# Five engine programs without a Block around them, and x's load behind GpSimd's first fills

## The chip, the cores and the metric

The kernel runs on one core of a Trainium2 chip. The metric is the device time of one execution in microseconds (us), and lower is better. A core has five engines that run their own instruction streams and meet only at semaphores: TensorE (PE; its weight loads are shown as PEld), VectorE (DVE), ScalarE (ACT), GpSimd (POOL) and SyncE (SP). SP and ACT also issue DMAs, each on a queue of its own (q1 and q10 in the profile); both queues are served by the same 16 DMA engines.

## What is computed

One decode step of a transformer block for 4 sequences, with a layer norm in front of two branches that run side by side and are added to x:

```python
def reference(A_x, A_k_cache, A_v_cache, A_wq, A_wo, B_x, B_w_gate, B_w_up, B_w_down):
    x = A_x                                  # (4, 1, 512)
    xn = _layernorm(x, axis=-1)
    # attention: 32 query heads, 8 key/value heads, the last 4096 of 16384 cache rows
    #   o = softmax((xn @ wq) . k * Dh**-0.5) . v ; return o @ wo
    # feed-forward: (silu(xn @ w_gate) * (xn @ w_up)) @ w_down
    return x + _A_ref(xn, A_k_cache, A_v_cache, A_wq, A_wo) + _B_ref(xn, B_w_gate, B_w_up, B_w_down)
```

All inputs are bfloat16. The parts of the two caches that are read are 32 MB each; the five weight matrices come to some 13 MB.

## The kernel before

**Staging.** The weights WQ, WG, WU, WD and WO have buffers of their own. The keys of one key/value head (4 sequences of 4096 rows, 4 MB) go into one buffer KB in two halves, the values into one buffer VB. There is one KB and one VB, so head r+1 can be loaded only where head r has been used.

**SP, the loads (L238 to L269).** SP issues WQ, WG, WU, then for each of the 8 heads the two halves of K (L245) and V (L250), WD after the first head (L263), at last WO in four parts (L253). A half of K waits until PE has transposed the same half of the head before (`s_tr`), V until PE has finished the product with the values of the head before (`s_pv`). At the end SP waits for the result (`s_y`), issues two of the four output DMAs, and waits until all four have landed (`wait_ge(d_out, 64)`, L269).

**POOL, the constants (L183 to L236).** POOL fills 17 tiles (L185 to L201), drains (L202), turns some of them into an identity, masks and selectors (`select`, L205), and raises `s_const` (L226); then it fills a few more and raises `s_zero` (L236).

**ACT (L271 to L297).** ACT issues the load of x (L273), takes the square root for the layer norm (L275), waits for `s_const`, issues four small loads of x in another layout (X4, L278), which are first used by the last addition, and then works through the heads: copies of transposed keys (L283) and exponentials (L286). It issues the other two output DMAs (L297).

**DVE (L299 to L377).** DVE waits for x, does the layer norm (L302 to L316, raising `s_xn`), copies the transposed x (L318) and the query (L320), does the feed-forward's activation (L362 to L368), then in each head copies of transposed keys (L330), maxima (L336) and the sums, and at the very end the addition of x (L377), which raises `s_y`.

**PE (L379 to L529).** PE waits for `s_const` and `s_xn`, transposes the normed x (L385), then waits for WQ and makes the query (L392), waits for WG and WU and makes gate and up (L399). Then comes a loop over the 8 heads: 16 chunks of transposed keys (L414) with the scores of the chunk two before (L427), the maximum and its shift (L434, L439), and the product with the values (L450, L455). In all heads but the first, extra matmuls without a use (`spin`, L467) stand between these steps. After the loop come the down projection and the output projection (L473, L477).

**The Block.** The five programs stand in one `with nc.Block() as block:` (L181). What the program makes of it: in front of each engine's instructions a branch to that engine's part, behind them a branch to a common end (line L181 in the profile), and in that end a barrier: each engine drains and counts up one semaphore, POOL waits until all four others have done so and releases them. A barrier of the same form stands ahead of the five programs (line L543); it belongs to the program's set-up and not to the Block.

Of the kernel before, what the change touches and what calls it, by code (L numbers as in the profile page):

```python
# [5 lines left out]
ALU = mybir.AluOpType  # L6
ACT = mybir.ActivationFunctionType
AX = mybir.AxisListType


def bass_parallel_sum__sliding_block_cached__swiglu_ffn__decode_kernel(
# [125 lines left out]
    d_v = sem("d_v")  # L137
    s_const = sem("s_const")
# [42 lines left out]
    with nc.Block() as block:  # L181

        @block.gpsimd  # L183
        def _(eng):
            eng.memset(ident[:], 0.0)  # L185
            eng.memset(I4[:], 0.0)
            eng.memset(ones[:], 1.0)
            eng.memset(own[:], 1.0)
            eng.memset(moff[:], 0.0)
            eng.memset(coff[:], 0.0)  # L190
            eng.memset(neg[:], 0.0)
            eng.memset(dq[:], 1.0)
            eng.memset(dr[:], 0.0)
            eng.memset(X4[:], 0.0)
            eng.memset(sel4[:], 0.0)
            eng.memset(guT[:].rearrange("p t b -> p (t b)"), 0.0)
            eng.memset(OP[:].rearrange("p t b -> p (t b)"), 0.0)
            eng.memset(sel[:], 0.0)
            eng.memset(head[:], 0.0)
            eng.memset(CM[:], 0.0)  # L200
            eng.memset(QT[:, HKV, :], 0.0)  # L201
            eng.drain()  # L202

            def select(t, pattern, op, fill, base, mult):
                eng.affine_select(t, t, pattern=pattern, compare_op=op, fill=fill, base=base,  # L205
                                  channel_multiplier=mult)
            select(I4[:], [[-1, B]], ALU.not_equal, 1.0, 0, 1)
            select(ident[:], [[-1, 128]], ALU.not_equal, 1.0, 0, 1)
            select(neg[:], [[-1, NH]], ALU.not_equal, -1.0, 0, 1)
            ownv = own[:].rearrange("k (j b) -> k j b", b=B)  # L210
            moffv = moff[:].rearrange("k (j b) -> k j b", b=B)
            coffv = coff[:].rearrange("k (b h) -> k b h", h=REP)
            select(ownv, [[0, NJ], [-REP, B]], ALU.is_ge, 0.0, 0, 1)
            select(moffv, [[0, NJ], [-REP, B]], ALU.is_ge, OFF, 0, 1)
            select(coffv, [[-REP, B], [0, REP]], ALU.is_ge, OFF, 0, 1)
            select(dq[:], [[-32, 4]], ALU.is_ge, 0.0, 0, 1)
            select(dr[:], [[-1, NR]], ALU.not_equal, 1.0, 0, 1)
            eng.drain()
            select(ownv, [[0, NJ], [REP, B]], ALU.is_ge, 0.0, REP - 1, -1)
            select(moffv, [[0, NJ], [REP, B]], ALU.is_ge, OFF, REP - 1, -1)  # L220
            select(coffv, [[REP, B], [0, REP]], ALU.is_ge, OFF, REP - 1, -1)
            select(dq[:], [[32, 4]], ALU.is_ge, 0.0, 31, -1)
            for a in range(1, 4):
                eng.drain()
                select(dr[:], [[-1, NR]], ALU.not_equal, 1.0, -32 * a, 1)
            eng.drain().then_inc(s_const, 1)  # L226

            for n in range(4):
                select(sel[:], [[-1, 32]], ALU.not_equal, 1.0, -32 * n, 1)
                select(head[:], [[0, 128]], ALU.not_equal, 1.0, -32 * n, 1)  # L230
                select(sel4[:], [[-1, B]], ALU.not_equal, 1.0, -32 * n, 1)
                eng.drain()
            eng.memset(dsum[:], 0.0)
            eng.memset(Osb[:], 0.0)
            eng.memset(P[:], 0.0)
            eng.drain().then_inc(s_zero, 1)  # L236

        @block.sync  # L238
        def _(eng):
            H = NT // 2  # L240

            def load_k(g, h):
                if g > 0:
                    eng.wait_ge(s_tr, NCH * (g - 1) + (h + 1) * NCH // 2)
                eng.dma_start(KB[:, h * H:(h + 1) * H, :], kv_ap(A_k_cache, g, h * H, (h + 1) * H)).then_inc(d_k[h], 16)  # L245

            def load_v(g):
                if g > 0:
                    eng.wait_ge(s_pv, g)
                eng.dma_start(VB[:], kv_ap(A_v_cache, g, 0, NT)).then_inc(d_v, 16)  # L250

            def load_wo(n, a, b):
                eng.dma_start(WO[:, a:b, :], wo_ap[:, a:b, :]).then_inc(d_wo[n], 16)  # L253

            eng.dma_start(WQ[:], wq_ap).then_inc(d_wq, 16)
            eng.dma_start(WG[:], wg_ap).then_inc(d_wg, 16)
            eng.dma_start(WU[:], wu_ap).then_inc(d_wu, 16)
            for g in range(HKV):
                load_k(g, 0)
                load_k(g, 1)  # L260
                load_v(g)
                if g == 0:
                    eng.dma_start(WD[:], wd_ap).then_inc(d_wd, 16)  # L263
            for q in range(4):
                load_wo(q, WOS[q], WOS[q + 1])
            eng.wait_ge(s_y, 1)
            for n in range(2):
                eng.dma_start(out_ap[n], y[32 * n:32 * n + B, :]).then_inc(d_out, 16)
            eng.wait_ge(d_out, 64)  # L269

        @block.scalar  # L271
        def _(eng):
            eng.dma_start(X[:], x_ap).then_inc(d_x, 16)  # L273
            eng.wait_ge(s_var, 1)
            eng.activation(st_std[:], st_var[:], ACT.Sqrt).then_inc(s_std, 1)  # L275
            eng.wait_ge(s_const, 1)
            for n in range(4):
                eng.dma_start(X4[32 * n:32 * n + B, :], x4_ap[n]).then_inc(d_x4, 16)  # L278

            def group(r):  # L280
                for n, c in enumerate(ACT_CH):
                    eng.wait_ge(s_tr, r * NCH + (c + 1))
                    eng.activation(KT[:, c % 4], kt_ps[c % 3], ACT.Copy).then_inc(s_ea, 1)  # L283
                for q in range(NB):
                    eng.wait_ge(s_mk, r * NB + (q + 1))
                    eng.activation(P[:, BT * q:BT * (q + 1), :], ps_S[q][:].rearrange("p (t n) -> p t n", n=NH),  # L286
                                   ACT.Exp, scale=SCALE).then_inc(s_p, 1)

            eng.wait_ge(s_gu, 1)
            eng.activation(ex[:], gate_ps.rearrange("p (t b) -> p t b", b=B), ACT.Exp, scale=-1.0).then_inc(s_ex, 1)  # L290
            with eng.Fori(0, HKV) as r:
                group(r)
            eng.wait_ge(s_e, 1)
            eng.activation(S2[:], acc4_ps[:], ACT.Copy).then_inc(s_ec, 1)  # L294
            eng.wait_ge(s_y, 1)
            for n in range(2, 4):
                eng.dma_start(out_ap[n], y[32 * n:32 * n + B, :]).then_inc(d_out, 16)  # L297

        @block.vector  # L299
        def _(eng):  # L300
            eng.wait_ge(d_x, 16)
            eng.tensor_reduce(st_sum[:], X[:], AX.X, ALU.add)  # L302
            eng.drain()
            eng.tensor_scalar(st_mean[:], st_sum[:], 1.0 / D, None, ALU.mult)
            eng.drain()
            eng.tensor_scalar(xc[:], X[:], st_mean[:, 0:1], None, ALU.subtract)
            eng.drain()
            eng.tensor_tensor(xsq[:], xc[:], xc[:], ALU.mult)
            eng.drain()
            eng.tensor_reduce(st_sum[:], xsq[:], AX.X, ALU.add)  # L310
            eng.drain()
            eng.tensor_scalar(st_var[:], st_sum[:], 1.0 / D, EPS, ALU.mult, ALU.add).then_inc(s_var, 1)
            eng.wait_ge(s_std, 1)
            eng.reciprocal(st_rstd[:], st_std[:])
            eng.drain()
            eng.tensor_scalar(xn[:], xc[:], st_rstd[:, 0:1], None, ALU.mult).then_inc(s_xn, 1)  # L316
            eng.wait_ge(s_xT, 1)
            eng.tensor_copy(XnT[:], xT_ps.rearrange("p (c b) -> p c b", b=B)).then_inc(s_xnT, 1)  # L318
            eng.wait_ge(s_q, 1)
            eng.tensor_copy(QT[:, 0:HKV].rearrange("p k (b h) -> p k b h", b=B),  # L320
                            q_ps.rearrange("p (k h b) -> p k b h", k=HKV, b=B))
            eng.drain()

            eng.tensor_copy(QC[:], QT[:, 0])

            def group(r, rest=None):
                for c in range(NCH):
                    if c not in ACT_CH:
                        eng.wait_ge(s_tr, r * NCH + (c + 1))
                        eng.tensor_copy(KT[:, c % 4], kt_ps[c % 3]).then_inc(s_ev, 1)  # L330
                    if c == 2 and rest:
                        rest()
# [37 lines left out]
            with eng.Fori(1, HKV) as r:  # L370
                group(r, lambda: norm(r - 1))
# [186 lines left out]
```

## Time and profile before

| | us |
|---|---|
| median of 3 runs | 197.28 (196.95 to 197.57) |
| the profiled execution, its own time | 196.62 |
| its span, first to last instruction | 194.9 |
| its mean granted TensorE clock | 0.982 of full speed |

The span and the rows of the trace are on one time scale, with zero at the first instruction. 196.62 - 194.9 = 1.72 us of the execution's own time lie ahead of the first or behind the last instruction that the trace shows. In the rows, DMA-issuing instructions stand under SPq and ACTq, a count of equal instructions behind "x", and in square brackets the idle time ahead of an instruction with what ended it. "us to landing" is counted from the issue to the last byte.

### The profile page before, as it was taken

The page shows a single profiled execution, that of the slowest core. Times are in us where ns is not written, and L with a number is a line of the kernel's source. Part 1 is how long each engine was busy: PE and PEld are TensorE (multiplying, and loading weights), DVE is VectorE, ACT ScalarE, POOL GpSimd, SP SyncE. Part 2 cuts the span into 40 slices and gives each one's busy share as a digit, 9 for nine tenths or more (in the row PEclk, how much of TensorE's full clock was granted, in tenths as well). Part 3 has the DMA queues.
Part 4 walks back from the last instruction along what each step waited for, and adds up shares of the span by engine and source line. Part 5 has one row for each costly group of instructions (what it writes and reads, how often), then busy time and mean ns, then how long its engine had stood idle before and what let it go on. Part 6 is the DMA issues. An engine that isn't in the chain of part 4 may idle for free.

```text
span 194.9 us, 8285 instructions
## 1 busy us (share of the span) xinstructions
PE 160.3 (82%) x3646; PEld 131.6 (68%) x3646; DVE 101.7 (52%) x217; ACT 61.1 (31%) x77; POOL 12.0 (6%) x51
## 2 busy tenths in 40 slices
PE   0137759958699979997999799979997999799984
PEld 0127759946698569856985597559756976697632
DVE  4200025870478348824882588258825882588230
ACT  2020002524064406440634063407340734073401
POOL 8870000000000000000000000000000000000000
PEclk9999999985999999999999999999999999999999
DMA  6999999999999999999999999999999999999991
GB/s 216 430 435 430 418 427 437 434 424 423 427 481 425 387 430 474 430 397 430 464 430 414 430 454 430 414 430 447 437 420 430 441 430 420 430 441 430 436 396 67
DMA packets 4688, 81.13 MB, mean 416 GB/s; under 512 B 580, under 2 KB 584, under 8 KB 968
## 3 DMA queue, kind: packets, MB, share of 16 engines
q1 hardware_dynamic: 4624, 81.01, 97.2%
q8 instruction: 6, 0.10, 0.2%
q10 hardware_dynamic: 56, 0.01, 0.0%
q14 instruction: 2, 0.02, 0.0%
HBM read 81.01 MB, written 0.00 MB: 416 GB/s over the span
## 4 chain that ended last, share of the span: by engine, by line
DMA 63%; PE 32%; DVE 2%; issue 1%; ACT 0%; SPq 0%; DVEq 0%
DMA kbuf<-in_A_k_cache_dram 52%; PE ps_kt L414 18%; DMA wu_sb<-in_B_w_up_dram 11%; PE ps_s L427 5%; PE ps_o L399 2%; PE ps_kt L467 2%; PE ps_s L473 1%; PE ps_o L463 1%; PE ps_o L450 1%; PE ps_o L462 1%; DVE kT L330 1%; PE ps_s L439 0%; PE ps_s L477 0%; DVE oP L374 0%; ACT s L294 0%
## 5 line engine op out<-in xcount | busy, mean ns | idle before, releaser
L414 PE MATMUL ps_kt<-ident,kbuf 128*128 128x128 bf16 x1024 | 76.5, 221 | 10.2 <-DMA kbuf<-in_A_k_cache_dram 8.2
L330 DVE COPY kT<-ps_kt 128x1024 bf16<-128x1024 bf16 x88 | 57.6, 686 | 21.6 <-PE ps_kt L414 21.6
L414 PEld LDWEIGHTS ps_kt<-ident,kbuf 128*128 128x128 bf16 x1024 | 59.2, 98 | 13.4 <-DMA kbuf<-in_A_k_cache_dram 13.4
L283 ACT ACTIVATE kT<-ps_kt 128x1024 bf16<-128x1024 bf16 x40 | 41.0, 1024 | 65.5 <-PE ps_kt L414 65.5
L427 PE MATMUL ps_s<-qC,kT 128*128 128x16 bf16 x1024 | 44.6, 170 | 3.1 <-DVE kT L330 2.1
L427 PEld LDWEIGHTS ps_s<-qC,kT 128*128 128x128 bf16 x1024 | 37.5, 97 | 4.6 <-DVE kT L330 4.1
L286 ACT ACTIVATE p<-ps_s 128x512 bf16<-128x512 f32 x32 | 16.5, 602 | 34.7 <-PE ps_s L439 34.7
L467 PE MATMUL ps_kt<-own,ones 128*128 128x512 bf16 x102 | 25.9, 380 | 0.0
L336 DVE TENSOR_REDUCE mx<-ps_s 128x16 f32<-128x512 f32 x32 | 22.0, 689 | 5.7 <-PE ps_s L427 3.6
L450 PEld LDWEIGHTS ps_o<-vbuf,p 128*32 128x32 bf16 x1024 | 17.8, 102 | 4.6 <-ACT p L286 4.6
L450 PE MATMUL ps_o<-vbuf,p 128*32 128x128 bf16 x1024 | 19.2, 228 | 0.3
L348 DVE COPY osb<-ps_o 128x128 f32<-128x128 f32 x8 | 2.3, 292 | 29.9 <-PE ps_o L455 29.9
L455 PE MATMUL ps_o<-p,ones 128*32 128x256 bf16 x64 | 17.0, 287 | 0.0
L467 PEld LDWEIGHTS ps_kt<-own,ones 128*128 128x128 bf16 x102 | 8.2, 98 | 8.2 <-issue 1.1
L439 PE MATMUL ps_s<-cm,own 128*128 128x512 bf16 x32 | 9.1, 411 | 1.0 <-DVE cm L345 1.0
L385 PE MATMUL ps_s<-i,xn 4*128 4x4 f32 x4 | 0.6, 261 | 9.2 <-POOLq L226 9.2
L385 PEld LDWEIGHTS ps_s<-i,xn 4*128 4x128 f32 x4 | 0.6, 206 | 9.2 <-POOLq L226 9.2
L455 PEld LDWEIGHTS ps_o<-p,ones 128*32 128x32 bf16 x64 | 6.5, 101 | 0.0
L439 PEld LDWEIGHTS ps_s<-cm,own 128*128 128x128 bf16 x32 | 2.6, 101 | 5.7 <-DVE cm L345 3.5
L392 PE MATMUL ps_s<-xnT,wq_sb 128*128 128x4 bf16 x128 | 3.6, 166 | 3.4 <-DMA wq_sb<-in_A_wq_dram 3.4
L392 PEld LDWEIGHTS ps_s<-xnT,wq_sb 128*128 128x128 bf16 x128 | 3.5, 104 | 3.5 <-issue 3.5
L362 DVE TENSOR_SCALAR ex<-ex 128x56 f32<-128x56 f32 x1 | 0.2, 192 | 9.1 <-ACT ex L290 9.1
(84 smaller groups left out, 77.4 us busy)
## 6 DMA issues: line engine op xcount, KB each, us to landing
kbuf<-in_A_k_cache_dram SPq DMA_DIRECT2D x16, 2048.0 KB, 14.1
vbuf<-in_A_v_cache_dram SPq DMA_DIRECT2D x8, 4096.0 KB, 16.5
wq_sb<-in_A_wq_dram SPq DMA_DIRECT2D x1, 4096.0 KB, 12.3
wo_sb<-in_A_wo_dram SPq DMA_DIRECT2D x1, 2816.0 KB, 22.6
wg_sb<-in_B_w_gate_dram SPq DMA_DIRECT2D x1, 1792.0 KB, 16.7
wu_sb<-in_B_w_up_dram SPq DMA_DIRECT2D x1, 1792.0 KB, 20.9
wd_sb<-in_B_w_down_dram SPq DMA_DIRECT2D x1, 1792.0 KB, 42.1
wo_sb<-in_A_wo_dram SPq DMA_DIRECT2D x1, 640.0 KB, 23.5
```

What stands on the lines that cost most here:

```text
L283: eng.activation(KT[:, c % 4], kt_ps[c % 3], ACT.Copy).then_inc(s_ea, 1)
L286: eng.activation(P[:, BT * q:BT * (q + 1), :], ps_S[q][:].rearrange("p (t n) -> p t n", n=NH), ACT.Exp, scale=SCALE).then_inc(s_p, 1)
L330: eng.tensor_copy(KT[:, c % 4], kt_ps[c % 3]).then_inc(s_ev, 1)
L336: eng.tensor_reduce(mx[:, q, :], ps_S[q][:].rearrange("p (t n) -> p n t", n=NH), AX.X, ALU.max)
L392: last = mm(q_ps[:, h * B:(h + 1) * B], WQ[:, c, h * Dh:(h + 1) * Dh], XnT[:, c, :], start=(c == 0 and h == 0), stop=(c == NC - 1), skip_g ...
L399: last = mm(o[:, t * B:(t + 1) * B], w[:].rearrange("p c (m t) -> p c t m", t=NF)[:, c, t, :], XnT[:, c, :], start=(w is WG and t == 0 and ...
L414: last = eng.transpose(kt_ps[c % 3][:, k, :], KB[:, CH * c + k, :], ident[:])
L427: last = mm(ps_S[q][:, NH * t:NH * (t + 1)], KT[:, c % 4, k, :], QC[:], start=(t == 0), stop=False, skip_group_check=True)
L439: mm(ps_S[q][:].rearrange("p (t n) -> p t n", n=NH), own[:], CM[:].unsqueeze(1).to_broadcast([128, BT, NH]), start=False, stop=True, skip_ ...
L450: mm(O_ps[32 * n:32 * n + 32, :], P[:, t:t + 2, :].rearrange("p t n -> p (t n)"), VB[:, t, :], start=(t < 4), stop=(t >= NT - 4), skip_gro ...
L455: last = mm(den_ps[32 * n:32 * n + 32, :], ones[:, 0:32], P[:, DT * e:DT * (e + 1), :].rearrange("p t n -> p (t n)"), start=False, stop=(e ...
L467: mm(ps_kt[k][:], ones[:], own[:].unsqueeze(1).to_broadcast([128, 4, 128]), skip_group_check=True)
```

## The change

The Block goes. Each engine's program becomes a plain function with the same body; the five are called one after another in the main program, in the order SP, POOL, ACT, DVE, PE. With the Block go its branches and the barrier at its end. The barrier of the set-up stays, and so does SP's last wait for the four output DMAs.

One wait is added: POOL's first drain, the one behind its 17 fills, raises a new semaphore `s_go`, and ACT waits for it before it issues the load of x. No other instruction, and no order on any engine, is changed. (The lines of the changed kernel are 2 to 5 lower than those of the kernel before.)

```diff
+    s_go = sem("s_go")
...
-    with nc.Block() as block:
-        @block.gpsimd
-        def _(eng):
+    def on_gpsimd(eng):
...
             eng.memset(QT[:, HKV, :], 0.0)
-            eng.drain()
+        eng.drain().then_inc(s_go, 1)
...
-        @block.scalar
-        def _(eng):
+    def on_scalar(eng):
+        eng.wait_ge(s_go, 1)
         eng.dma_start(X[:], x_ap).then_inc(d_x, 16)
...
+    on_sync(nc.sync)
+    on_gpsimd(nc.gpsimd)
+    on_scalar(nc.scalar)
+    on_vector(nc.vector)
+    on_tensor(nc.tensor)
```

More of the change, by code (lines that the diff above doesn't have):

```diff
@@ new lines, in on_sync, with load_k, load_v, load_wo @@
+    def on_sync(eng):
+        H = NT // 2
+        def load_k(g, h):
+            if g > 0:
+                eng.wait_ge(s_tr, NCH * (g - 1) + (h + 1) * NCH // 2)
+            eng.dma_start(KB[:, h * H:(h + 1) * H, :], kv_ap(A_k_cache, g, h * H, (h + 1) * H)).then_inc(d_k[h], 16)
+        def load_v(g):
+            if g > 0:
+                eng.wait_ge(s_pv, g)
+            eng.dma_start(VB[:], kv_ap(A_v_cache, g, 0, NT)).then_inc(d_v, 16)
+        def load_wo(n, a, b):
+            eng.dma_start(WO[:, a:b, :], wo_ap[:, a:b, :]).then_inc(d_wo[n], 16)
+        eng.dma_start(WQ[:], wq_ap).then_inc(d_wq, 16)
+        eng.dma_start(WG[:], wg_ap).then_inc(d_wg, 16)
+        eng.dma_start(WU[:], wu_ap).then_inc(d_wu, 16)
+        for g in range(HKV):
+            load_k(g, 0)
+            load_k(g, 1)
+            load_v(g)
+            if g == 0:
+                eng.dma_start(WD[:], wd_ap).then_inc(d_wd, 16)
+        for q in range(4):
+            load_wo(q, WOS[q], WOS[q + 1])
+        eng.wait_ge(s_y, 1)
+        for n in range(2):
+            eng.dma_start(out_ap[n], y[32 * n:32 * n + B, :]).then_inc(d_out, 16)
+        eng.wait_ge(d_out, 64)
@@ new lines, in on_scalar, with group @@
+    def on_scalar(eng):
+        eng.wait_ge(s_go, 1)
+        eng.dma_start(X[:], x_ap).then_inc(d_x, 16)
+        eng.wait_ge(s_var, 1)
+        eng.activation(st_std[:], st_var[:], ACT.Sqrt).then_inc(s_std, 1)
+        eng.wait_ge(s_const, 1)
+        for n in range(4):
+            eng.dma_start(X4[32 * n:32 * n + B, :], x4_ap[n]).then_inc(d_x4, 16)
+        def group(r):
+            for n, c in enumerate(ACT_CH):
+                eng.wait_ge(s_tr, r * NCH + (c + 1))
+                eng.activation(KT[:, c % 4], kt_ps[c % 3], ACT.Copy).then_inc(s_ea, 1)
+            for q in range(NB):
+                eng.wait_ge(s_mk, r * NB + (q + 1))
+                eng.activation(P[:, BT * q:BT * (q + 1), :], ps_S[q][:].rearrange("p (t n) -> p t n", n=NH),
+                               ACT.Exp, scale=SCALE).then_inc(s_p, 1)
+        eng.wait_ge(s_gu, 1)
+        eng.activation(ex[:], gate_ps.rearrange("p (t b) -> p t b", b=B), ACT.Exp, scale=-1.0).then_inc(s_ex, 1)
+        with eng.Fori(0, HKV) as r:
+            group(r)
+        eng.wait_ge(s_e, 1)
+        eng.activation(S2[:], acc4_ps[:], ACT.Copy).then_inc(s_ec, 1)
+        eng.wait_ge(s_y, 1)
+        for n in range(2, 4):
+            eng.dma_start(out_ap[n], y[32 * n:32 * n + B, :]).then_inc(d_out, 16)
@@ new lines, in on_vector, with group, norm @@
+    def on_vector(eng):
+        eng.wait_ge(d_x, 16)
+        eng.tensor_reduce(st_sum[:], X[:], AX.X, ALU.add)
+        eng.drain()
+        eng.tensor_scalar(st_mean[:], st_sum[:], 1.0 / D, None, ALU.mult)
+        eng.drain()
+        eng.tensor_scalar(xc[:], X[:], st_mean[:, 0:1], None, ALU.subtract)
+        eng.drain()
+        eng.tensor_tensor(xsq[:], xc[:], xc[:], ALU.mult)
+        eng.drain()
+        eng.tensor_reduce(st_sum[:], xsq[:], AX.X, ALU.add)
+        eng.drain()
+        eng.tensor_scalar(st_var[:], st_sum[:], 1.0 / D, EPS, ALU.mult, ALU.add).then_inc(s_var, 1)
+        eng.wait_ge(s_std, 1)
+        eng.reciprocal(st_rstd[:], st_std[:])
+        eng.drain()
+        eng.tensor_scalar(xn[:], xc[:], st_rstd[:, 0:1], None, ALU.mult).then_inc(s_xn, 1)
+        eng.wait_ge(s_xT, 1)
+        eng.tensor_copy(XnT[:], xT_ps.rearrange("p (c b) -> p c b", b=B)).then_inc(s_xnT, 1)
+        eng.wait_ge(s_q, 1)
+        eng.tensor_copy(QT[:, 0:HKV].rearrange("p k (b h) -> p k b h", b=B),
+                        q_ps.rearrange("p (k h b) -> p k b h", k=HKV, b=B))
+        eng.drain()
+        eng.tensor_copy(QC[:], QT[:, 0])
+        def group(r, rest=None):
+            for c in range(NCH):
+                if c not in ACT_CH:
+                    eng.wait_ge(s_tr, r * NCH + (c + 1))
+                    eng.tensor_copy(KT[:, c % 4], kt_ps[c % 3]).then_inc(s_ev, 1)
+                if c == 2 and rest:
+                    rest()
+                for q in range(NB):
+                    if c == min(NCH - 1, (q + 1) * NCH // NB + 1):
+                        eng.wait_ge(s_sc, r * NB + (q + 1))
+                        eng.tensor_reduce(mx[:, q, :], ps_S[q][:].rearrange("p (t n) -> p n t", n=NH), AX.X, ALU.max)
+            eng.drain()
+            eng.tensor_reduce(m16[:], mx[:].rearrange("p q n -> p n q"), AX.X, ALU.max).then_inc(s_m, 1)
+            eng.tensor_copy(QC[:], QT[:, r + 1] if isinstance(r, int) else QT[:, bass.ds(r + 1, 1)].rearrange("p o n -> p (o n)"))
+            eng.wait_ge(s_mt, r + 1)
+            eng.tensor_tensor(junk[:], mT_ps, moff[:], ALU.add)
+            eng.drain()
+            eng.tensor_reduce(M[:], junk[:], AX.X, ALU.max)
+            eng.drain()
+            eng.scalar_tensor_tensor(CM[0:NH, :], neg[:], M[:, 0:1], coff[:], ALU.mult, ALU.add).then_inc(s_cm, 1)
+            eng.wait_ge(s_pv, r + 1)
+            eng.tensor_copy(Osb[:], O_ps)
+            eng.tensor_reduce(dsum[:], den_ps.rearrange("p (t n) -> p n t", n=NH), AX.X, ALU.add).then_inc(s_dn, 1)
+        def norm(r):
+            eng.wait_ge(s_fin, r + 2)
+            eng.reciprocal(den[:], D2_ps)
+            eng.drain()
+            eng.tensor_tensor(on[:], O2_ps, den[:], ALU.mult)
+            eng.drain()
+            o = OT[:, :, r] if isinstance(r, int) else OT[:, :, bass.ds(r, 1)].rearrange("p b o h q -> p b (o h) q")
+            eng.tensor_tensor(o, on[:].rearrange("p (b h) -> p b h", b=B).unsqueeze(3).to_broadcast([128, B, REP, 4]),
+                              dq[:].unsqueeze(1).unsqueeze(1).to_broadcast([128, B, REP, 4]), ALU.mult).then_inc(s_nrm, 1)
+        eng.wait_ge(s_ex, 1)
+        eng.tensor_scalar(ex[:], ex[:], 1.0, None, ALU.add)
+        eng.drain()
+        eng.reciprocal(ex[:], ex[:])
+        eng.drain()
+        eng.tensor_tensor(gs[:], gate_ps.rearrange("p (t b) -> p t b", b=B), ex[:], ALU.mult)
+        eng.drain()
+        eng.tensor_tensor(guT[:, :, 0:B], up_ps.rearrange("p (t b) -> p t b", b=B), gs[:], ALU.mult).then_inc(s_guT, 1)
+        group(0)
+        with eng.Fori(1, HKV) as r:
+            group(r, lambda: norm(r - 1))
+        norm(HKV - 1)
+        eng.wait_ge(s_pm, 1)
+        eng.tensor_copy(OP[:, :, 0:B].rearrange("p r b -> p b r"), perm_ps.rearrange("p (b r) -> p b r", b=B)).then_inc(s_pc, 1)
+        eng.wait_ge(s_acc, 1)
+        eng.wait_ge(d_x4, 64)
+        eng.tensor_tensor(y[:], acc_ps, X4[:], ALU.add).then_inc(s_y, 1)
@@ new lines, in on_tensor, with transposes, scores, maxima @@
+    def on_tensor(eng):
+        mm = eng.matmul
+        eng.wait_ge(s_const, 1)
+        eng.wait_ge(s_xn, 1)
+        for c in range(NC):
+            last = eng.transpose(xT_ps[:, c * B:(c + 1) * B],
+                                 xn[:].rearrange("b (p c) -> b c p", c=NC)[:, c, :], I4[:])
+        last.then_inc(s_xT, 1)
+        eng.wait_ge(s_xnT, 1)
+        eng.wait_ge(d_wq, 16)
+        for c in range(NC):
+            for h in range(HQ):
+                last = mm(q_ps[:, h * B:(h + 1) * B], WQ[:, c, h * Dh:(h + 1) * Dh], XnT[:, c, :],
+                          start=(c == 0 and h == 0), stop=(c == NC - 1), skip_group_check=True)
+        last.then_inc(s_q, 1)
+        for w, d, o in ((WG, d_wg, gate_ps), (WU, d_wu, up_ps)):
+            eng.wait_ge(d, 16)
+            for t in range(NF):
+                for c in range(NC):
+                    last = mm(o[:, t * B:(t + 1) * B],
+                              w[:].rearrange("p c (m t) -> p c t m", t=NF)[:, c, t, :], XnT[:, c, :],
+                              start=(w is WG and t == 0 and c == 0), stop=(c == NC - 1),
+                              skip_group_check=True)
+        last.then_inc(s_gu, 1)
+        eng.sem_inc(s_p, NB)
+        eng.sem_inc(s_nrm, 1)
+        eng.sem_inc(s_dn, 1)
+        eng.wait_ge(s_zero, 1)
+        eng.wait_ge(s_guT, 1)
+        def transposes(r, c):
+            if c % (NCH // 2) == 0:
+                eng.wait_ge(d_k[c // (NCH // 2)], r * 16 + 16)
+            for k in range(CH):
+                last = eng.transpose(kt_ps[c % 3][:, k, :], KB[:, CH * c + k, :], ident[:])
+            last.then_inc(s_tr, 1)
+        def scores(r, c):
+            q = c * CH // BT
+            if c % (NCH // NB) == 0:
+                eng.wait_ge(s_p, r * NB + (q + 1))
+            if c in ACT_CH:
+                eng.wait_ge(s_ea, r * len(ACT_CH) + (ACT_CH.index(c) + 1))
+            else:
+                eng.wait_ge(s_ev, r * (NCH - len(ACT_CH)) + (c + 1 - sum(a < c for a in ACT_CH)))
+            for k in range(CH):
+                t = CH * c + k - BT * q
+                last = mm(ps_S[q][:, NH * t:NH * (t + 1)], KT[:, c % 4, k, :], QC[:],
+                          start=(t == 0), stop=False, skip_group_check=True)
+            if (c + 1) % (NCH // NB) == 0:
+                last.then_inc(s_sc, 1)
+        def maxima(r):
+            eng.wait_ge(s_m, r + 1)
+            eng.transpose(mT_ps, m16[:], ident[:]).then_inc(s_mt, 1)
+        def shift(r):
+            eng.wait_ge(s_cm, r + 1)
+            for q in range(NB):
+                mm(ps_S[q][:].rearrange("p (t n) -> p t n", n=NH), own[:],
+                   CM[:].unsqueeze(1).to_broadcast([128, BT, NH]),
+                   start=False, stop=True, skip_group_check=True).then_inc(s_mk, 1)
+        def pv(r):
+            for t in range(NT):
+                n = t % 4
+                if t % BT == 0:
+                    eng.wait_ge(s_p, r * NB + (NB + t // BT + 1))
+                if t % BT == BT - 1 and t < NT - 1:
+                    eng.wait_ge(s_p, r * NB + (NB + t // BT + 2))
+                mm(O_ps[32 * n:32 * n + 32, :], P[:, t:t + 2, :].rearrange("p t n -> p (t n)"), VB[:, t, :],
+                   start=(t < 4), stop=(t >= NT - 4), skip_group_check=True)
+                if t % DT == DT - 1:
+                    e = t // DT
+                    n = e % 4
+                    last = mm(den_ps[32 * n:32 * n + 32, :], ones[:, 0:32],
+                              P[:, DT * e:DT * (e + 1), :].rearrange("p t n -> p (t n)"),
+                              start=False, stop=(e >= NT // DT - 4), skip_group_check=True)
+            last.then_inc(s_pv, 1)
+        def fin(r):
+            eng.wait_ge(s_dn, r + 1)
+            mm(D2_ps, head[:], dsum[:], start=True, stop=True, skip_group_check=True)
+            mm(O2_ps, Osb[:], sel[:, 0:NH], start=True, stop=True, skip_group_check=True).then_inc(s_fin, 1)
+        def spin(n, k=2):
+            for _ in range(n):
+                mm(ps_kt[k][:], ones[:], own[:].unsqueeze(1).to_broadcast([128, 4, 128]),
+                   skip_group_check=True)
+        HD = D // 4
+        def acc4(n, left, right, start, stop):
+            return mm(acc4_ps[32 * n:32 * n + 32, :], left, right, start=start, stop=stop, skip_group_check=True)
+        def acc(left, right, start, stop):
+            for n in range(4):
+                last = mm(acc_ps[32 * n:32 * n + B, :], left, right[:, HD * n:HD * (n + 1)],
+                          start=start, stop=stop, skip_group_check=True)
+            return last
+        def down():
+            eng.wait_ge(d_wd, 16)
+            eng.wait_ge(s_guT, 1)
+            for t in range(NF):
+                acc4(t % 4, guT[:, t, :], WD[:, t, :], t < 4, False)
+        with eng.Fori(0, HKV) as r:
+            for c in range(NCH):
+                transposes(r, c)
+                if c == 2:
+                    fin(r)
+                if c >= 2:
+                    scores(r, c - 2)
+            scores(r, NCH - 2)
+            scores(r, NCH - 1)
+            with eng.If(r > 0):
+                spin(5)
+            maxima(r)
+            with eng.If(r > 0):
+                spin(5)
+            shift(r)
+            eng.wait_ge(s_nrm, r + 1)
+            eng.wait_ge(d_v, r * 16 + 16)
+            pv(r)
+            with eng.If(r > 0):
+                spin(4)
+        down()
+        fin(HKV)
+        spin(2)
+        eng.wait_ge(s_nrm, HKV + 1)
+        for b in range(B):
+            last = mm(perm_ps[:, NR * b:NR * (b + 1)], OT[:, b].rearrange("p k h q -> p (k h q)"), dr[:])
+        last.then_inc(s_pm, 1)
+        spin(2, 1)
+        eng.wait_ge(s_pc, 1)
+        for q in range(4):
+            eng.wait_ge(d_wo[q], 16)
+            for e in range(WOS[q], WOS[q + 1]):
+                if e < WOE:
+                    last = acc4(e % 4, OP[:, e, :], WO[:, e, :], False, e >= WOE - 4)
+                else:
+                    last = acc(OP[:, e, 0:B], WO[:, e, :], e == WOE, e == NR - 1)
+            if WOS[q + 1] == WOE:
+                last.then_inc(s_e, 1)
+            if q == 1:
+                eng.wait_ge(s_ec, 1)
+                acc(sel4[:], S2[:], False, False)
+        last.then_inc(s_acc, 1)
```

354 lines of the change are left out of this document (47 added, 307 removed).

## The prediction, made before the changed kernel had run

> **What bounds the kernel now.** I read the page's transfers first, since the slices of its span are nearly all 9 there, then the chain of work that ended last.
>
> ```profile
> span 194.9 us, 8285 instructions
> DMA  6999999999999999999999999999999999999991
> q1 hardware_dynamic: 4624, 81.01, 97.2%
> DMA 63%; PE 32%; DVE 2%; issue 1%; ACT 0%; SPq 0%; DVEq 0%
> kbuf<-in_A_k_cache_dram SPq DMA_DIRECT2D x16, 2048.0 KB, 14.1
> wd_sb<-in_B_w_down_dram SPq DMA_DIRECT2D x1, 1792.0 KB, 42.1
> ```
>
> SP's queue (q1) keeps the 16 DMA engines busy for 97.2% of the span with 81 MB, and transfers hold 63% of the chain. In order of time the chain shows how it starts and how it goes over to PE (start, length, what):
>
> ```profile
> 0.73 0.07 issue
> 0.80 0.41 SPq L255
> 1.22 0.06 issue
> 1.28 0.41 SPq L256
> 1.69 0.05 issue
> 1.74 20.93 DMA wu_sb<-in_B_w_up_dram
> ...
> 35.13 16.23 DMA kbuf<-in_A_k_cache_dram
> ...
> 153.55 14.13 DMA kbuf<-in_A_k_cache_dram
> 167.73 1.51 PE ps_kt L414 x24
> ...
> 192.44 0.29 DVE y_sb L377
> ```
>
> So the time is the start of the stream (0.80), the stream until the last head's first half of K lands (153.55 + 14.13 = 167.68), a PE tail of 25 us to the addition at L377 (ends 192.73), and what follows that. The change touches only the two ends and the work that has to hide in the stream's first 50 us. The end, from SP's waits and from the instructions of L181, the Block's line (ns, then first and last start):
>
> ```profile
> SPq L181 <- DMA out_dram<-y_sb: 1.1, 1, 1.1
> SPq L181 <- PEq L181: 0.2, 1, 0.2
> L181 SPq COMPARE_BRANCH  x1: 33/33/33, 194.5 to 194.5; - x1
> L181 SPq DRAIN  x1: 13/13/13, 194.7 to 194.7; - x1
> L181 POOLq EVENT_SEMAPHORE  x2: 17/17/17, 194.7 to 194.8; - x2
> L181 PEldq EVENT_SEMAPHORE  x1: 51/51/51, 194.8 to 194.8; - x1
> ```
>
> At 194.5 the outputs have landed and SP's waiting branch ends. All that comes behind it, up to 194.9, is the Block's exit: a drain on SP, two semaphore steps on POOL, the release of all.
>
> **The change part by part.**
>
> *The exit barrier goes.* SP's wait for the outputs stays, now as the program's last instruction: it ends at 194.5 + 0.03. The span then ends there: 194.9 - 194.53 = 0.37 us less. Nothing covers this stretch, as every engine stands in it, so all of it is gained. The other engines' drains of L181 lay earlier, under SP's wait of 1.1 us, and are worth nothing.
>
> *The branches at the entry go.* The chain has 0.07 us between the release of the set-up's barrier and SP's first load, a step in which the branch would lie. Between SP's next loads, where there is no branch, it has 0.06 and 0.05. The branch is therefore worth 0 to 0.02 us (0.07 - 0.05); I take 0.02. The stream starts that much earlier, and everything in it moves along.
>
> *The load of x waits.* What it costs depends on when x lands and on who then waits.
>
> ```profile
> 0.80 0.57 ACTq L273 DMA_DIRECT2D x_sb<-in_A_x_dram  x1
> 2.54 0.67 DVE L302 TENSOR_REDUCE st_sum<-x_sb 4x1 f32<-4x512 bf16 x1 [2.54 <-DMA x_sb<-in_A_x_dram]
> 3.30 0.10 POOL L201 MEMSET qT<- 128x16 bf16 x1
> 6.28 0.47 DVE L316 TENSOR_SCALAR xn<-xc,st_rstd 4x512 f32<-4x512 f32 x1
> 9.20 1.32 ACTq L278 DMA_DIRECT2D x<-in_A_x_dram  x4
> 9.22 0.64 PE L385 MATMUL ps_s<-i,xn 4*128 4x4 f32 x4 [9.22 <-POOLq L226]
> 9.90 0.17 DVE L318 CAST xnT<-ps_s 128x16 bf16<-128x16 f32 x1 [3.14 <-PE ps_s L385]
> 13.26 3.55 PE L392 MATMUL ps_s<-xnT,wq_sb 128*128 128x4 bf16 x128 [3.40 <-DMA wq_sb<-in_A_wq_dram]
> 18.01 3.52 PE L399 MATMUL ps_o<-xnT,wg_sb 128*128 128x4 bf16 x56 [1.20 <-DMA wg_sb<-in_B_w_gate_dram]
> 22.71 0.46 PE L399 MATMUL ps_o<-xnT,wu_sb 128*128 128x4 bf16 x5 [1.18 <-DMA wu_sb<-in_B_w_up_dram]
> 49.81 0.53 SPq L250 DMA_DIRECT2D vbuf<-in_A_v_cache_dram  x1
> ```
>
> Now x is issued at 0.80 and is there at 2.54, 1.74 us later, ahead of the stream. POOL's last fill ends at 3.40, so the issue moves to about 3.5, into the stream. The lower bound for the landing is 3.5 + 1.74 = 5.2. For a small load on ACT's queue within the stream the nearest row is X4 (L278), which ACT issues from 9.20 on. The transfers by queue, in the windows 9.2 to 12.6, 12.6 to 14.2 and 14.2 to 17.0 in that order, and last in 5.0 to 9.0, where only WQ runs (packets, MB, share of 16 engines):
>
> ```profile
> q1 hardware_dynamic: 61, 1.28, 87.6%
> ...
> q1 hardware_dynamic: 50, 0.69, 101.2%
> q10 hardware_dynamic: 9, 0.00, 0.5%
> ...
> q10 hardware_dynamic: 23, 0.00, 0.7%
> ...
> q1 hardware_dynamic: 58, 1.90, 110.1%
> ```
>
> ACT's queue (q10) has no packet for 3.4 us after X4's issue, then 9 up to 14.2 and 23 up to 17.0, while SP's queue still holds everything behind WQ. A packet of WQ occupies an engine for 4.0 x 16 x 1.10 / 58 = 1.21 us. So x begins about 3.4 us after its issue, at 6.9, and its completion has to go past another packet or two of 1.21: 8.1 to 9.3. I take 9; the upper bound is WQ's own end, where X4 surely was served, some 13.
>
> From x to the query: the norm takes 6.75 - 2.54 = 4.21, transposes and copy 10.07 - 9.22 = 0.85, hand-overs 0.1, together 5.16. The query could start at 9 + 5.16 = 14.2 instead of 13.26. PE sits idle 1.20 ahead of WG and 1.18 ahead of WU, and so takes 2.4 us of lateness before the first matmul of WU moves. With 14.2 - 13.26 = 0.9 it is gone ahead of WG. Cost: 0. A landing up to 10.5 (13.26 - 5.16 + 2.4) leaves even WU where it is.
>
> What lies behind the wait on ACT: its square root (its input comes later by the same amount), the X4 loads, whose tile is used at 192.44 only, and the table for the exponential, first needed after the last matmul of WU. Each moves back by some 6 us at most and none is asked for by then.
>
> If x lands later than 10.5, PE moves one for one, and the stream hides it: it needs the next V (issued at 49.81, after the first head's last product) only when the loads queued ahead are through. The second head's first half of K lands at 35.13 + 16.23 = 51.36, its other 2048 KB need 2048 / 4096 of what 9.8 us bring (81.01 MB in 0.972 x 194.9 us is 428 GB/s), 4.9 us, until 56.3. With 1.7 us for an issue to take effect, V may be issued at 54.6: 4.8 us of cover. The landing from which the kernel pays is 10.5 + 4.8 = 15.3.
>
> By the Trainium skill, page "DMA: Bandwidth & Descriptors", section "Queues, rings and completion order", a DMA engine changes from one queue to another only after a packet of some 9 to 17 descriptors, so x would stand behind all of WQ. It would then land near 13.7, with the sum unchanged and only some 1.6 us of cover left. The rows speak against that grain in part: 9 packets of ACT's queue stand among only 50 of SP's on 16 engines.
>
> **Sum.** 0.37 + 0.02 + 0 = 0.39 us off the profiled execution's 196.62: 196.2. That execution was 0.66 us faster than the median of the runs, so the forecast for a median is 197.28 - 0.39 = **196.9**, 0.2% faster. A measurement of this kernel tells about 0.3% (0.59 us) from no change, so this one counts as "same".
>
> **The rivals.**
>
> *More than the span shows.* 1.72 us of the execution lie outside its span. With the barrier all five engines leave together at 194.8; without it POOL is done at about 15, PE and DVE at 192.7, and whatever each does behind its program no longer stands behind SP's wait. No row shows this stretch. Its bounds are 0 and 1.72; half of it, 0.86, gives 197.28 - 0.39 - 0.86 = 196.0. For it: four engines end early. Against it: nothing shows that the stretch lies at the end at all. The Trainium skill speaks against it: its page "Runtime: NRT & Kernel Launch", section "The launch sequence", has a barrier of all engines first in what follows a program. By that page the early engines would only wait there, and the time would be that of the sum; no run here shows that stretch.
>
> *The barrier is not gone but replaced.* If something behind the program takes the Block's place and costs as much, the time stays at 197.3. For it: the same five engines have to be known done in any case. Against it: the same would have been paid in addition before.
>
> *x starves, and the kernel gets slower.* If ACT's queue is not served before SP's earlier loads are through, x lands with WG (18.0) or WU (22.7). From 15.3 on each microsecond counts: 2.7 us (199.6) or 7.4 us (204.3). For it: X4 had no packet for 3.4 us. Against it: X4 was served by 17.0, while WU, K, V and WD were still queued.
>
> **How the numbers follow.** The sum's case 0.50, more than the span shows 0.32, a barrier replaced 0.10, x starving 0.08. "Faster" by over 0.3% (below 196.7) is most of the second case (0.28) and a fifth of the first by the scatter of medians (runs from 196.95 to 197.57): 0.38. "Slower" is x starving and a little scatter, 0.09. The rest, 0.53, is "same". The range reaches from the second case's 196.0 to 197.5, where the replaced barrier with scatter lies; it leaves out the starving x and the far end of the 1.72 us.
>
> **What would show it.** Right: the span at 194.5, its last instruction SP's wait for the outputs; SP's first load within 0.1 us of the barrier's release; x's issue at 3.5 and the first reduction between 8 and 10; the query at about 14.2, WG's and WU's matmuls at 18.0 and 22.7 as before; V of the second head at 49.8. Wrong: a first matmul of WU later than 22.7 with the K stream moved too, a gap in the DMA slices near 56 us, or a time that falls by much more than the span does.

## The result, and the profile after

The changed kernel takes **196.0 us** (median of 8 runs, 195.87 to 196.32) beside 196.84 us for the kernel before (median of 8 runs, 196.66 to 197.57). The ratio is 0.9952, with a 95% interval of 0.9939 to 0.9966: 0.5% faster. The forecast was 196.9 from a kernel before at 197.28, 0.39 us less, which it counted as too little to tell from no change. The gain measured is 0.84 us and clear of the scatter; the time is that of the rival "More than the span shows".

The page of the changed kernel, the lines that answer to those of before:

```profile
span 194.7 us, 8274 instructions
DMA  6999999999999899999999999999999999999992
q1 hardware_dynamic: 4624, 81.01, 97.3%
DMA 55%; PE 36%; DVE 5%; issue 1%; POOLq 1%; ACT 1%; POOL 0%; DVEq 0%
wd_sb<-in_B_w_down_dram SPq DMA_DIRECT2D x1, 1792.0 KB, 42.4
```

The stream is the same: as many packets, as many bytes, the engines filled as before. Only the chain's shares look different (63% DMA before). Its pieces in order of time say why (start, length, what):

```profile
1.55 1.92 POOLq L200
3.49 5.95 DMA x_sb<-in_A_x_dram
9.47 0.67 DVE st_sum L298
...
13.23 1.80 DVE xn L312
15.17 0.62 PE ps_s L380 x4
16.05 3.58 PE ps_s L387 x128
19.62 6.73 PE ps_o L394 x112
26.89 0.50 DVE ex L360
28.32 2.74 PE ps_kt L409 x24
...
35.53 15.84 DMA kbuf<-in_A_k_cache_dram
51.41 1.51 PE ps_kt L409 x24
```

The chain no longer begins with SP's loads up to WU (1.74 + 20.93 = 22.67 before). It runs through POOL's fills, x, the norm and the query into the matmuls of gate and up. That looks as if x had become the bound, but PE begins the first head at 28.32 (28.26 before), and the second head's K lands at 35.53 + 15.84 = 51.37, against 51.36. A chain shows who came last at each meeting, not by how much.

The end, from SP's waits and from the line of SP's last wait (ns, first and last start):

```profile
SPq L266 <- DMA out_dram<-y_sb: 1.1, 1, 1.1
```

```profile
L266 SPq EVENT_SEMAPHORE  x1: 17/17/17, 194.7 to 194.7; - x1
```

SP's wait for the outputs is the last instruction, and the span ends with it. Behind it nothing is recorded. Each run gives its time and its span. For the 8 runs after, time less span is 1.28 us in the mean (1.24 to 1.37); for the 21 runs of the kernel before that were taken beside the first experiments it is 1.73 (1.68 to 1.84), with a median span of 195.1 against 194.75. So the 0.84 us are **some 0.35 to 0.4 within the span and 0.45 outside it**.

### The profile page after: what moved, and what is told of

Its sections match the earlier page's. It is cut to its first block, busy times and chain, and to the rows that moved or that the text cites. A ratio compares the mean times of both kernels' runs of the same rounds, so it can differ in the third digit from the quotient of the medians.

```text
span 194.7 us, 8274 instructions
## 1 busy us (share of the span) xinstructions
PE 160.0 (82%) x3646; PEld 131.5 (68%) x3646; DVE 103.0 (53%) x217; ACT 61.1 (31%) x77; POOL 11.9 (6%) x51
## 4 chain that ended last, share of the span: by engine, by line
DMA 55%; PE 36%; DVE 5%; issue 1%; POOLq 1%; ACT 1%; POOL 0%; DVEq 0%
DMA kbuf<-in_A_k_cache_dram 52%; PE ps_kt L409 18%; PE ps_s L422 5%; PE ps_o L394 3%; DMA x_sb<-in_A_x_dram 3%; PE ps_s L387 2%; PE ps_kt L462 2%; PE ps_s L468 1%; PE ps_o L458 1%; PE ps_o L445 1%; PE ps_o L457 1%; POOLq L200 1%; DVE xn L312 1%; DVE kT L326 1%; PE ps_s L434 0%
## 5 line engine op out<-in xcount | busy, mean ns | idle before, releaser
L298 DVE TENSOR_REDUCE st_sum<-x_sb 4x1 f32<-4x512 bf16 x1 | 0.7, 674 | 9.5 <-DMA x_sb<-in_A_x_dram 9.5
L429 PEld LDWEIGHTS ps_kt<-ident,m 128*16 128x16 bf16 x8 | 0.7, 86 | 4.8 <-DVE m L334 4.8
```

## The experiments

**Theory A**, formed from the result: behind an engine's last instruction there is work that the trace doesn't record; the Block's barrier made all engines begin it together at the very end, and without it four of them do it under SP's wait. **Rivals**: the gain outside the span comes from the entry (branches) or from the load of x; the branches inside the program made it slower; the gain is only in the span and the rest is scatter.

The first three experiments tell the two parts of the change apart, and try to bring the barrier's effect back without a Block. The wait alone, in the kernel before:

```diff
+    s_go = sem("s_go")
...
-            eng.drain()
+            eng.drain().then_inc(s_go, 1)
...
+            eng.wait_ge(s_go, 1)
             eng.dma_start(X[:], x_ap).then_inc(d_x, 16)
```

> The Block is kept and only the wait of x's load for POOL's first drain is added. Theory (the Block's end alone counts: 0.37 us inside the span, and some 0.45 us outside it because four engines leave early): no change, 196.8 us, span 194.9 to 195.1, time outside the span 1.7 us. Rival (the wait of x is part of the gain, by relieving POOL, ACT or the first loads): 0.2 to 0.5 us faster than before, with the time outside the span or the end of the stream changed.

Measured: 196.86 us, ratio 0.9997 (0.9988 to 1.0006), outside the span 1.75. The wait for POOL's fills costs nothing that can be measured, though x landed at 9.24 instead of 2.54.

The other part alone, the changed kernel without the wait:

```diff
-    s_go = sem("s_go")
...
-        eng.drain().then_inc(s_go, 1)
+        eng.drain()
...
-        eng.wait_ge(s_go, 1)
```

> The Block is gone and x is loaded at once, as before. Theory (the Block's end alone counts): as fast as the changed kernel, 196.0 us, or up to 0.2 us faster if the late x has shifted the end of the stream; span 194.5 to 194.7, time outside the span 1.27 us. Rival (the wait of x is part of the gain): 196.2 to 196.5 us.

Measured: 195.95 us, 0.9954 (0.9941 to 0.9968), outside 1.27. The whole gain belongs to the Block.

The changed kernel in which the four other engines wait at their ends until SP has seen the outputs:

```diff
+    s_end = sem("s_end")
...
         eng.wait_ge(d_out, 64)
+        eng.sem_inc(s_end, 1)
...
+        eng.wait_ge(s_end, 1)      (at the end of POOL, ACT, DVE and PE)
```

> The changed kernel, with POOL, ACT, DVE and PE made to wait at their end for a signal that SP gives when the outputs have landed: all five leave together again, but with no Block, no branch and no drain. Theory (early leavers): the time outside the span goes back to 1.7 us, the span grows by the signal's 0.1 us, 196.5 us in all. Rival (the Block's own branches, drains and longer programs cost the time outside the span): it stays at 1.27 us and the kernel at 196.1 us.

Measured: 196.69 us, 0.9985 (0.9972 to 0.9999), outside 1.79. There is no Block in this kernel, and so neither the Block's branches nor its barrier; its engines only leave late. Its span, from the same line of SP:

```profile
core 0 of [0], span 194.9 us
...
L269 SPq EVENT_SEMAPHORE  x1: 17/17/17, 194.8 to 194.8; - x1
```

The median span is 194.9, 0.15 more than after, and outside it the time is 0.51 more. So what lies outside the span depends on when the engines finish. The entry cannot be the cause: it is the same in this kernel as in the changed one.

**Which engine?** Each of the four held alone, with the diff above cut to one engine's wait:

> The changed kernel with POOL alone made to wait at its end for SP's signal. Theory A (one engine's end takes long, and it is POOL's): 196.5 to 196.7 us, time outside the span 1.7 us. Theory B (another engine's): 196.0 to 196.1 us and 1.3 us. Theory C (every engine adds its share): some 196.2 us and 1.4 us.

> The changed kernel with ACT alone made to wait at its end for SP's signal. Theory A (one engine's end takes long, and it is ACT's): 196.5 to 196.7 us, time outside the span 1.7 us. Theory B (another engine's): 196.0 to 196.1 us and 1.3 us. Theory C (every engine adds its share): some 196.2 us and 1.4 us.

> The changed kernel with DVE alone made to wait at its end for SP's signal. Theory A (one engine's end takes long, and it is DVE's): 196.5 to 196.7 us, time outside the span 1.7 us. Theory B (another engine's): 196.0 to 196.1 us and 1.3 us. Theory C (every engine adds its share): some 196.2 us and 1.4 us.

> The changed kernel with PE alone made to wait at its end for SP's signal. Theory A (one engine's end takes long, and it is PE's): 196.5 to 196.7 us, time outside the span 1.7 us. Theory B (another engine's): 196.0 to 196.1 us and 1.3 us. Theory C (every engine adds its share): some 196.2 us and 1.4 us.

Then all but POOL, to see whether the prices add up or the largest counts; and last the wait for the outputs given to POOL, with SP done after its last output DMA:

```diff
+        eng.wait_ge(d_out, 64)     (at the end of POOL)
...
-        eng.wait_ge(d_out, 64)     (at the end of SP)
```

> The changed kernel with ACT, DVE and PE made to wait for SP's signal at their end, POOL free to leave. Theory (the latest end counts): PE's time outside the span, 1.54 us, 196.3 us. Rival (the shares add up, 1.28 + 0.12 + 0.10 + 0.26): 1.76 us, 196.6 us.

> The changed kernel with the last wait, for the four output DMAs, on POOL in place of SP; SP ends with its last output DMA. Theory (each engine has a stretch of its own behind its last instruction, POOL's the longest, and the latest end counts): time outside the span 1.75 to 1.8 us, 196.5 us. Rival (what costs is a second engine released by a signal, not which engine is last): 1.3 us and 196.0 us.

Measured, with the kernels above:

| who finishes with the outputs | time, us | ratio to before | span, median | time less span, mean |
|---|---|---|---|---|
| SP alone (after) | 196.0 | 0.9952 (0.9939 to 0.9966) | 194.75 | 1.28 |
| SP and DVE | 196.21 | 0.9951 (0.9936 to 0.9966) | 194.8 | 1.39 |
| SP and ACT | 196.07 | 0.9951 (0.9935 to 0.9967) | 194.7 | 1.41 |
| SP and PE | 196.34 | 0.9973 (0.9959 to 0.9986) | 194.8 | 1.54 |
| SP, ACT, DVE and PE | 196.35 | 0.9974 (0.9964 to 0.9984) | 194.85 | 1.54 |
| SP and POOL | 196.64 | 0.9974 (0.996 to 0.9988) | 194.8 | 1.79 |
| POOL alone | 196.47 | 0.9975 (0.9961 to 0.9989) | 194.7 | 1.78 |
| all five, held by SP | 196.69 | 0.9985 (0.9972 to 0.9999) | 194.9 | 1.79 |

The rows stand beside different runs of the kernel before, whose median moved between 196.84 and 197.01 and its span between 195.1 and 195.3, while its time less span stayed at 1.72 to 1.73. So the last column is the one to compare; in it 0.02 us, as between DVE and ACT, is no difference.

Three things follow. **The latest end decides**: three engines together give 1.54, which is PE's price alone, and all give 1.79, which is POOL's. **The price depends on which engine is last**: from 1.28 for SP to 1.79 for POOL. **No signal is needed**: with POOL waiting for the same DMAs in SP's place, the last instruction of the program is the same wait at the same time (next fence, from the kernel with POOL alone), and the time outside the span is 0.50 us longer.

```profile
core 0 of [0], span 194.7 us
engine op xcount: duration ns min/median/max, first and last start us, forms
L235 POOLq EVENT_SEMAPHORE  x1: 17/17/17, 194.7 to 194.7; - x1
```

This line stands at 194.7 on POOL, as L266 stands at 194.7 on SP in the changed kernel. Equal spans, different times: the trace doesn't show it, only the times beside it do.

**Does x's wait have a price later on?** The prediction put the landing from which the kernel pays at 15.3. Two kernels hold x's load longer, until WG and until WQ have landed:

```diff
-        eng.wait_ge(s_go, 1)
+        eng.wait_ge(d_wg, 16)      (in the other kernel: d_wq)
```

> The changed kernel with x's load waiting until WG has landed (about 17.9 us) in place of POOL's drain. The prediction's cover: x lands at about 23.5 us, 8.2 us beyond 15.3, and the kernel takes 8 to 9 us longer, 204 to 205 us, with the stream dry ahead of the second head's K and V. Rival (the stream's cover is wider than computed, since PE makes up time in the first head): under 4 us longer.

> The changed kernel with x's load waiting until WQ has landed (about 13 us); x should land near 17.8 us. The prediction's cover, which ends at a landing of 15.3: 2.5 us longer, 198.5 us. One for one with the run that loads x behind WG (205.3 us at a landing of 22.5): 4.6 us longer, 200.6 us. The issue of the second head's V alone, from the times of the changed kernel's trace: 3.4 us longer, 199.4 us.

Measured, with two runs each: 205.32 us behind WG (1.043, 1.0405 to 1.0455) and 201.45 us behind WQ (1.0237, 1.0215 to 1.0259). The landings and the first transposes of keys, first behind WG, then behind WQ:

```profile
22.55 0.67 DVE L298 TENSOR_REDUCE st_sum<-x_sb 4x1 f32<-4x512 bf16 x1 [22.55 <-DMA x_sb<-in_A_x_dram]
39.98 2.74 PE L409 MATMUL ps_kt<-ident,kbuf 128*128 128x128 bf16 x24 [1.98 <-DVE guT L364]
```

```profile
18.65 0.67 DVE L298 TENSOR_REDUCE st_sum<-x_sb 4x1 f32<-4x512 bf16 x1 [18.65 <-DMA x_sb<-in_A_x_dram]
36.08 2.74 PE L409 MATMUL ps_kt<-ident,kbuf 128*128 128x128 bf16 x24 [1.98 <-DVE guT L364]
```

3.90 us later in landing are 3.90 later on PE and 3.87 in time, so both lie where each microsecond counts. Back from 201.45 to 196.0 is 5.45 us. If each microsecond counts all the way back, the paying point is a landing of 18.65 - 5.45 = **13.2**, not 15.3; this is an estimate, as no kernel has x land between 10.4 and 18.6. Where the stream runs dry is seen in the windows (window and length, PE, PEld, DVE, ACT, POOL busy with their counts, granted clock, DMA share, GB/s), behind WQ first, then in the changed kernel:

```profile
42.00:48.00 6.00, 6.00 (x120) 6.00 (x118) 4.26 (x7) 3.07 (x3) 0.00 (x0) 1.00 0.71 274
...
54.00:60.00 6.00, 5.96 (x166) 5.08 (x164) 1.42 (x4) 2.06 (x4) 0.00 (x0) 0.72 0.66 249
```

```profile
42.00:48.00 6.00, 3.46 (x50) 1.70 (x51) 2.50 (x7) 1.53 (x4) 0.00 (x0) 0.59 1.03 436
...
54.00:60.00 6.00, 6.00 (x153) 5.92 (x151) 4.93 (x11) 4.10 (x4) 0.00 (x0) 1.00 1.05 446
```

It runs dry twice: already in 42 to 48 (29 GB/s from 45 to 46), and again in 54 to 60 (none from 58 to 59). SP's issues of the kernel behind WQ name the loads:

```profile
44.96 5.72 SPq L242 DMA_DIRECT2D kbuf<-in_A_k_cache_dram  x2
58.58 0.54 SPq L247 DMA_DIRECT2D vbuf<-in_A_v_cache_dram  x1
```

The second head's K is issued at 44.96 (35.53 after), when almost nothing is queued any more, and V at 58.58.

**Is GpSimd's last fill in x's way?** In the changed kernel the last step of the norm meets POOL's fill of P (from the timeline):

```profile
12.93 1.82 POOL L233 MEMSET p<- 128x2064 bf16 x1
13.23 1.79 DVE L312 TENSOR_SCALAR xn<-xc,st_rstd 4x512 f32<-4x512 f32 x1
```

That step took 0.47 before. The last kernel fills P early, behind the first drain:

```diff
         eng.drain().then_inc(s_go, 1)
+        eng.memset(P[:], 0.0)
...
-        eng.memset(P[:], 0.0)
```

> The changed kernel with POOL's fill of P moved from its end to right behind its first drain. Theory (in the changed kernel the norm's last step took 1.79 us in place of 0.47 because it runs beside that fill): 0.47 to 0.6 us for that step, the query about 1.3 us earlier, at 14.7; the time stays at 196.0 us, since the stream covers it. Rival (a late x or the loads in flight slow VectorE): the step stays at 1.8 us.

Measured: 196.08 us, 0.9967 (0.9953 to 0.9981), outside the span 1.24. Its timeline:

```profile
10.19 0.68 DVE L298 TENSOR_REDUCE st_sum<-x_sb 4x1 f32<-4x512 bf16 x1 [10.19 <-DMA x_sb<-in_A_x_dram]
...
13.96 0.47 DVE L312 TENSOR_SCALAR xn<-xc,st_rstd 4x512 f32<-4x512 f32 x1
...
15.45 3.57 PE L387 MATMUL ps_s<-xnT,wq_sb 128*128 128x4 bf16 x128 [0.27 <-DVE xnT L314]
```

The step is back at 0.47, and from x to the query it is 15.45 - 10.19 = 5.26 us instead of 16.05 - 9.47 = 6.58. The time is that of the changed kernel, as the query has cover. None of these kernels is clearly faster than the changed one.

## Why the prediction was wrong

**The step that failed** is the sum's first line: the profiled execution's 1.72 us outside the span were carried over unchanged, and only the 0.37 us of exit barrier inside the span were counted. The held engines show in its place that this stretch shrinks by 0.45 us, from 1.73 to 1.28, when POOL, PE, ACT and DVE may finish early. The prediction named that mechanism as a rival with a chance of 0.32 and priced it at half of 1.72, 0.86; its real size is half of that. That the time came out at the rival's 196.0 all the same is luck: the kernel before was at 196.84 over all eight runs, and not at the 197.28 of the three runs from which the prediction subtracted.

What spoke against the rival was a rule: by the Trainium skill, page "Runtime: NRT & Kernel Launch", section "The launch sequence", all engines first meet in a barrier behind the program. From it the prediction inferred that early engines would only wait there and the time outside the span would stay. That inference does not hold: POOL leaving last costs 0.5 us more than SP leaving last at an equal span. Either each engine does something of its own ahead of such a meeting, or the meeting takes longer when certain engines come last; the runs do not tell these apart.

Point by point:

- **Exit barrier, 0.37 us in the span: right.** SP's wait is the last instruction. From the start of the last addition to the span's end it takes 2.46 us before (192.44 to 194.9) and 2.06 after (192.64 to 194.7), 0.40 less; the medians of the spans, 195.1 before and 194.75 after, differ by 0.35. The span of the profiled execution ends at 194.7 instead of the 194.5 forecast because that addition starts 0.20 later. With one execution each, it starts at 192.44 and 192.50 in the two kernels without the wait and at 192.51 to 192.89 in the ten with the wait for POOL, so the wait may cost some 0.1 to 0.2 us there; the medians (196.86 against 196.84 with the Block, 196.0 against 195.95 without it) are too close to show it.
- **Branches at the entry, 0.02: too small to be seen.** SP's first load is issued at 0.80 in both traces.
- **x's landing, 9 us: right.** It was issued at 3.49, as forecast, and the first reduction began at 9.47. By the Trainium skill, page "DMA: Bandwidth & Descriptors", section "Queues, rings and completion order", a DMA engine goes over to another queue only after a packet of some 9 to 17 descriptors. The prediction's estimate from that was a landing near 13.7; the trace does not agree, with 3.49 + 5.95 = 9.44.
- **From x to the query, 5.16 us: too small.** It took 6.58, since the norm taken from before (4.21) did not meet the fill of P. The query began at 16.05 instead of 14.2, and WG's matmuls at 19.48 instead of 18.0; in WU the lateness was used up but for 0.13 (22.84 against 22.71), so there was no cost to be measured, as forecast.
- **V of the second head at 49.8: it was 50.97**, without a consequence (next row, SP's issues of the changed kernel).

```profile
50.97 0.54 SPq L247 DMA_DIRECT2D vbuf<-in_A_v_cache_dram  x1
```

- **Paying point, 15.3: too late, by some 2 us if the estimate of 13.2 holds.** That PE follows x one for one from 10.5 is about right: the transposes stand 17.43 us behind the landing in both late kernels, and 28.26 - 17.43 = 10.8. The stream's cover of 4.8 would then be 13.2 - 10.8 = 2.4. The prediction looked at V alone; in the late kernels the stream is short of the second head's K first. Behind WQ, V's issue also comes 58.58 - 36.08 = 22.50 us after the first transposes, 0.95 more than before (49.81 - 28.26 = 21.55). How much each of the two takes from the cover stays open. With x at 9.5 none of it was needed.
- **"Barrier replaced"** is refuted by the 0.9954 of the Block's removal alone, **"x starves"** by x's landing at 9.44, before WQ's at some 13.

**What stays open**: what an engine does in its stretch. The trace has no record there, and the runs only give how much longer it is than SP's.

## What to carry to other kernels

When a barrier or a wait at the end goes, look at which engine finishes last, and let the wait for the outputs stand on the one with the shortest way out (here SP): the span showed only about half of the gain. A price read inside the span can miss a part as long as the time and the span differ by a stretch that no record explains; measure that stretch by holding single engines. A wait that turns up in the chain of work has cost nothing if the times behind the next meeting are those of before.

## What the runs showed of the hardware

**Engines leave at different prices.** Time less span was 1.28 us with SP last, 1.39 with DVE, 1.41 with ACT, 1.54 with PE, 1.78 to 1.79 with POOL.

**A step on VectorE waited for a fill on GpSimd.** The last step of the norm took 1.79 us beside POOL's fill of P (12.93 to 14.75) and 0.47 without it. It ended at 15.02, 0.27 us behind the fill, which is less than its own 0.47: it stood for nearly all of the fill. By the Trainium skill, page "SBUF — State Buffer", section "Terms", the two share a port pair that one holds for a full instruction while the other is blocked; for this step the trace agrees. Not every pair of instructions waits: the norm's second reduction took 0.67 us from 11.84 on, as it did in the kernel behind WQ where POOL was done, and the three selects on POOL beside it kept their 0.20 to 0.29.

**PE's pace in the first head is not the same in every execution.** From the first transposes of keys to SP's issue of the next K took 6.87 us before, 7.21 after, 8.61 in the changed kernel without the wait, and 8.88 in both kernels with a late x. The edits do not explain it: with POOL held it took 8.88 (28.22 to 37.10) and with ACT held 6.58 (28.22 to 34.80), and these two differ only at their ends. Beside each other, the windows of the kernel before and of the changed kernel without the wait, 32 to 34 us:

```profile
32.00:34.00 2.00, 2.00 (x51) 2.00 (x50) 0.69 (x1) 1.18 (x2) 0.00 (x0) 1.00 0.76 328
```

```profile
32.00:34.00 2.00, 2.00 (x33) 2.00 (x31) 0.00 (x0) 1.02 (x1) 0.00 (x0) 1.00 0.83 360
```

PE is busy all the time in both, but finishes 51 matmuls in the one and 33 in the other, at a granted clock of 1.00. Groups of 8 transposes take 1.01 us in the second of the two until 36.1 and 0.61 from 36.96 on:

```profile
35.11 1.01 PE L407 MATMUL ps_kt<-ident,kbuf 128*128 128x128 bf16 x8
36.17 0.74 PE L407 MATMUL ps_kt<-ident,kbuf 128*128 128x128 bf16 x8
36.96 0.61 PE L407 MATMUL ps_kt<-ident,kbuf 128*128 128x128 bf16 x8
```

In this kernel the stream covers it. In the kernels with a late x it may be part of what is paid. Why the pace changes when it does stays open.
